# Weights of a later stage differenced during the attention, eight buffers for w3, and a reordered tail

## The chip, the core and the metric

The kernel runs on one core of a Trainium2 chip. The metric is the device time of one execution in microseconds (us). The engines named below are TensorE (PE: matmuls and transposes; its weight loads are shown as PEld), VectorE (DVE), ScalarE (ACT), GpSimd (POOL) and SyncE (SP), which issues every DMA that this text speaks of. Each engine runs its own instructions in the order in which they were laid down; between engines semaphores make an instruction wait for its operands and for buffers to come free.

## The reference

Causal attention with a bias is followed by two feed-forward blocks. Only the shape of the sums matters here:

```python
# q, k, v: 4 batches, 8 heads, 576 tokens, head_dim 64; T = 2304 tokens, DM = 512, DF = 1024
attn = softmax(where(causal, -1e9, q @ k.T / 8 + minimum(bias(s), 0)))
x = (attn @ v).reshape(2304, 512)
a, b = x @ w1, x @ w2                 # 512 x 1024 each
x2 = (a * b @ w3) @ w_out             # w3: 1024 x 1024, w_out: 1024 x 512
h = x2 @ w_in                         # second block, w_in: 512 x 1024
e = exp(h - max(h)); solu = h * e / (sum(e) + 1e-9)
ln = (solu - mean(solu)) / sqrt(var(solu) + 1e-6) * g_ln
out = ln @ w_out2                     # 1024 x 512
```

## The kernel before, in words

**Numbers.** A product in nearly full fp32 is made of three matmuls of the type fp32r: each operand is written as a high word (`hi`, an ACT copy, line 95) and a low word (`lo`, a DVE or POOL subtraction, line 100), and PE adds high·high, high·low and low·high. The weights arrive as raw 64-bit floats. One *job* is one piece of 128x512: SP loads 512 KB of raw bits into a `stage` buffer (L406), `to_f32` converts them (one ACT operation, L362, and three of DVE, L368, L369 and L373), and then the piece is either split into words (`split_w`) or, for weights that are needed late, written to scratch memory in HBM (`wf_scr`, `spill_job`). `pump(n)` emits n jobs and issues as many further loads as there are free stage buffers: 2 in the attention, 4 behind it.

**Stages.** (1) The attention goes over 32 heads in the list `steps`; PE's idle time there is filled by parts of `ab_unit`, which makes a = xw1 and b = xw2 for a batch and one slice of the columns, and `g = a*b` by DVE (L346), which is spilled to `g_scr`. The table `PUMP` says how many jobs belong to each step: first w1 and w2, then 16 spill jobs (8 of w_in, 8 of w_out2, the latter scaled by g_ln). (2) A stretch in which only the last batch's `ab_unit`s run (16 of them) and in which the 8 jobs of the first w_out and the first 6 of the 16 jobs of w3 are emitted (`AP3`). (3) **M**: since nothing stands between w3 and w_out, the product M = w3·w_out is formed once: 8 `m_unit`s of 24 matmuls each, 128x512 (L603), then split into `MH` and `ML`. A new pool of PSUM banks is opened ahead of M, so the first matmul of M waits until the last `g` has been read out of the old pool's banks. The remaining jobs of w3 are emitted between the units (`AM`); each `m_unit` needs two jobs' pieces `w3h` and `w3l`, of which five buffers each exist. (4) Chunks of 256 tokens, c = 0 to 8: x2 = g·M (L685), h from seven products by a Strassen-like scheme (L715), softmax and layer norm on ACT and DVE, transposes, and `out_unit` (24 matmuls of L809 each, 128x512).

**The operands of h.** The seven products take seven 128x512 operands of each half of w_in: the pieces B11, B21 and B22 themselves, and T1 = B12 - B11, T2 = B22 - T1, T3 = B22 - B12 and T4 = B21 - T2. Before the change these are made *during M*: `i_step` is called after each `m_unit`; the spilled pieces of w_in are loaded back (`wf`, 3 buffers), POOL does the subtractions (`wsub`, L868) into `s_m` and `a_m`, ACT makes the high words and DVE or POOL the low ones. With two halves that is 14 high words, 10 low words on DVE, 4 low words on POOL and 8 subtractions on POOL.

**The tail.** In most chunks the layer norm's result is transposed by DMA (`turn`, `join`). In the last one (tiles 16 and 17) PE does it: `tr2` is two groups of four transposes (L799), each followed by a high and a low word. `out_unit` of tiles 14 to 17 stands around them.

**What sets the order.** The program is written in one order, and a scheduler that simulates a timeline lays each engine's instructions down from it, so that what is written behind M can come out among M's instructions. SP's queue too is in one fixed order: a load that waits for its buffer holds what stands behind it.

Of the kernel before, what the change touches and what calls it, by code (L numbers as in the profile page):

```python
# [20 lines left out]
CW = 512  # L21
# [5 lines left out]
def tile_attention_moe(  # L27
# [44 lines left out]

    wf_scr = [dram.tile([128, CW], F32, name=f"wf_scr{i}") for i in range(16)]
    g_scr = [dram.tile([KF, 128, S], F32, name=f"g_scr{n}") for n in range(B)]
# [361 lines left out]

    def spill_job(i):
        src = w_in[i // 2 * 128:i // 2 * 128 + 128, i % 2 * 1024:i % 2 * 1024 + 1024] if i < 8 else wo2[(i - 8) * 128:(i - 7) * 128]

        def conv(raw):  # L440
            t = at.tile([128, CW], F32, tag="cst", bufs=2, name="cst")
            to_f32(raw, None, t)
            if i >= 8:
                nc.scalar.activation(out=t, in_=t, func=AF.Copy, scale=gln[:, i - 8:i - 7])
            nc.sync.dma_start(out=wf_scr[i], in_=t)

        jobs.append((src, conv))

    zz = r0.tile([128, HS], F32, tag="a_sb", bufs=2, name="zz")
# [53 lines left out]
    for f in range(KF):  # L505
        for w in range(2):
            wab_job(f, w)
    for i in range(16):
        spill_job(i)

# [6 lines left out]
    PD, FS = 10, 0.5  # L517
    PUMP = {3: 1, 5: 1, 6: 1, 10: 2, 11: 2, 12: 2, 13: 2, 14: 2, 15: 2, 16: 1, 18: 1, 19: 1, 20: 1, 21: 1, 22: 1, 23: 1, 24: 1, 25: 1, 26: 1, 27: 1, 28: 1, 29: 1, 30: 1, 31: 1, 32: 1, 33: 1}
    fill = []
# [71 lines left out]
    def w3_job(f, i):  # L591
        def dst():
            m_st[f, i] = [mp.tile([128, 4, 128], F32R, tag=f"w3{x}", bufs=5, name=f"w3{x}") for x in "hl"]
            return [flat(t) for t in m_st[f, i]]

        w_job(w3L[f, :, 1024 * i:1024 * i + 1024], dst)
# [105 lines left out]
    def x2_second(c):  # L702
# [5 lines left out]
        words(3, 7, s_m)  # L708

    def h_mm(ps, x, w, first):  # L710
        XH, XL = (t[:, XO[x]] for t in XW)
        WH, WL = IT[w]
        for k in range(2):
            for x_, w_ in ((XH, WH), (XH, WL), (XL, WH)):
                nc.tensor.matmul(  # L715
                    ps, x_[:, k], w_[:, k],
                    start=first and k == 0 and x_ is XH and w_ is WH, stop=k == 1 and x_ is XL, skip_group_check=not first,
                )
# [131 lines left out]
    wf = {}  # L850
    WORDER = [(0, 1), (0, 0), (2, 1), (2, 0), (1, 1), (1, 0), (3, 1), (3, 0)]
    WSRC = [2 * c + h for c, h in WORDER] + list(range(8, 16))

    def wf_load(i):
        if i < 16:
            wf[i] = wpool.tile([128, CW], F32, tag="wf", bufs=3, name="wf")
            nc.sync.dma_start(out=wf[i], in_=wf_scr[WSRC[i]])

    def i_words(n, j, src, eng):
        h_, l_ = (t[:, j] for t in IT[n])  # L860
        hi(h_, src)
        lo(l_, src, h_, eng)

    s_f = s_m.rearrange("p a b c -> p (a b c)")
    t1_, t2_, t3_ = s_f[:, 0:HD], s_f[:, HD:2 * HD], a_m.rearrange("p a t -> p (a t)")

    def wsub(dst, a, b):
        nc.gpsimd.tensor_tensor(out=dst, in0=a, in1=b, op=ALU.subtract)  # L868

    def i_step(f):  # L870
        j, s_ = divmod(f, 4)
        b = 4 * j
        if s_ == 0:
            wsub(t1_, wf[b], wf[b + 1])
            i_words("B11", j, wf[b + 1], V)
            wf_load(b + 3)
        elif s_ == 1:
            wsub(t2_, wf[b + 2], t1_)
            wsub(t3_, wf[b + 2], wf[b])
            i_words("T1", j, t1_, V)  # L880
            wf_load(b + 4)
        elif s_ == 2:
            i_words("B22", j, wf[b + 2], V)
            wsub(t1_, wf[b + 3], t2_)
            i_words("T3", j, t3_, G)
            wf_load(b + 5)
        else:
            i_words("B21", j, wf[b + 3], V)
            i_words("T2", j, t2_, G)
            i_words("T4", j, t1_, V)  # L890
            wf_load(b + 6)

    load_g(0)
    for i in range(3):
        wf_load(i)
    load_g(1)
    for f in range(nm[0], KF):
        m_unit(f)
        pump(AM[f])
        i_step(f)  # L900
        if f == 5:
            split_g(0)
# [7 lines left out]
    x2_second(0)  # L910
    split_g(1)
    load_g(2)
    x2_half(1, 0)
    p3 = None
    for c in range(NCH):
# [3 lines left out]
        if c == 0:  # L919
            for k in range(8):  # L920
                hi(OH[:, k], wf[8 + k])
                lo(OL[:, k], wf[8 + k], OH[:, k])
                wf_load(11 + k)
            wp.close()
            p3 = ctx.enter_context(tc.tile_pool(name="p3", bufs=1, side="right"))
# [76 lines left out]
```

## Time and profile before

| | |
|---|---|
| time, median of 3 runs | 752.63 us (750.18 to 755.14) |
| the profiled execution: its own time | 749.91 us |
| its span in the profile | 748.0 us |
| mean granted clock of PE over the span | 0.987 |
| PE busy | 719.9 us (96%) |
| DVE busy | 506.4 us (68%) |
| ACT busy | 468.4 us (63%) |
| POOL busy | 120.6 us (16%) |

The profile is one execution; its time stands 2.7 us under the median of the runs, and 1.9 us of it lie outside the span. In the span, stage (2) takes from 343 to 394.7 us, M from 394.7 to 451.0 us, the chunks the rest; the last `out_unit`s end at 744.2 us. A busy share is an average over stages with different limits.

### The profile page before, as it was taken

The page shows a single profiled execution, that of the slowest core. Times are in us where ns is not written, and L with a number is a line of the kernel's source. Part 1 is how long each engine was busy: PE and PEld are TensorE (multiplying, and loading weights), DVE is VectorE, ACT ScalarE, POOL GpSimd, SP SyncE. Part 2 cuts the span into 40 slices and gives each one's busy share as a digit, 9 for nine tenths or more (in the row PEclk, how much of TensorE's full clock was granted, in tenths as well). Part 3 has the DMA queues.
Part 4 walks back from the last instruction along what each step waited for, and adds up shares of the span by engine and source line. Part 5 has one row for each costly group of instructions (what it writes and reads, how often), then busy time and mean ns, then how long its engine had stood idle before and what let it go on. Part 6 is the DMA issues. An engine that isn't in the chain of part 4 may idle for free.

```text
span 748.0 us, 13033 instructions
## 1 busy us (share of the span) xinstructions
PE 719.9 (96%) x4682; PEld 626.5 (84%) x4682; DVE 506.4 (68%) x1255; ACT 468.4 (63%) x985; POOL 120.6 (16%) x114
## 2 busy tenths in 40 slices
PE   8889998999999999999999869999999999999997
PEld 5567978878889889989998649998888988888875
DVE  7977878998767677425985975566747366564651
ACT  4987878888876787523644535466656465564642
POOL 5032313232221231000002620000000000000000
PEclk9999999999999999999999979999999999999999
DMA  4744645567665653104757514143334152313301
GB/s 112 182 122 100 191 135 162 174 178 211 182 181 181 181 164 114 72 32 167 239 190 260 175 56 127 56 93 78 85 85 99 43 127 72 84 29 57 67 32 43
DMA packets 78100, 92.37 MB, mean 123 GB/s; under 512 B 41226, under 2 KB 52490, under 8 KB 78036
## 3 DMA queue, kind: packets, MB, share of 16 engines
q1 hardware_dynamic: 78036, 91.54, 43.2%
q8 instruction: 37, 0.61, 0.3%
q14 instruction: 27, 0.22, 0.1%
HBM read 57.47 MB, written 18.57 MB: 102 GB/s over the span
## 4 chain that ended last, share of the span: by engine, by line
PE 70%; DVE 4%; issue 2%; DMA 1%; ACT 1%; SPq 0%; POOLq 0%; DVEq 0%; ACTq 0%
PE x L685 13%; PE o L809 12%; PE b L326 11%; PE a L326 11%; PE hX L715 5%; PE av L298 3%; PE hZ L715 3%; PE tr L265 2%; PE m L603 2%; PE sc L178 2%; PE hW L715 2%; PE hY L715 2%; PE sc L179 2%; DMA stage<-in_w_dram 1%; DVE w3l L100 1%
## 5 line engine op out<-in xcount | busy, mean ns | idle before, releaser
L196 ACT ACTIVATE P<-P,STAT 128x576 f32<-128x576 f32 (+4 forms) x160 | 88.3, 554 | 34.4 <-DVE STAT L192 33.9
L100 POOL TENSOR_TENSOR QK<-qk,QK 64x1152 fp32r<-64x1152 f32 x24 | 66.5, 2774 | 169.7 <-ACT QK L95 152.5
L685 PE MATMUL x<-gl,MH 128*128 128x256 f32 x288 | 80.2, 279 | 0.0
L685 PE MATMUL x<-gh,ML 128*128 128x256 f32 x288 | 80.2, 279 | 0.0
L685 PE MATMUL x<-gh,MH 128*128 128x256 f32 x288 | 80.0, 279 | 0.0
L192 DVE CUSTOM_DVE_ANT_0 P<-sc,wmask 128x576 f32<-128x576 f32 (+4 forms) x160 | 70.7, 479 | 5.9 <-PE sc L170 3.2
L326 PE MATMUL a<-xT0h,W 128*128 128x288 f32 x256 | 59.2, 304 | 0.7 <-ACT a_sb L338 0.7
L326 PE MATMUL b<-xT0h,W 128*128 128x288 f32 x256 | 57.3, 298 | 1.5 <-DVE STAT L192 0.8
L779 DVE COPY lt<-turned 128x2048 uint16<-128x2048 uint16 x16 | 22.6, 1414 | 51.7 <-DMA turned<-half 51.7
L326 PE MATMUL a<-xT1h,W 128*128 128x288 f32 x256 | 57.2, 298 | 0.0
L809 PE MATMUL o<-OH,lh 128*128 128x512 f32 x144 | 57.1, 397 | 0.0
L809 PE MATMUL o<-OH,ll 128*128 128x512 f32 x144 | 57.0, 396 | 0.0
L809 PE MATMUL o<-OL,lh 128*128 128x512 f32 x144 | 56.9, 395 | 0.0
L326 PE MATMUL b<-xT1h,W 128*128 128x288 f32 x256 | 56.5, 294 | 0.0
L685 PEld LDWEIGHTS x<-gl,MH 128*128 128x128 f32 x288 | 54.0, 188 | 1.3
L685 PEld LDWEIGHTS x<-gh,MH 128*128 128x128 f32 x288 | 54.1, 188 | 1.1
L685 PEld LDWEIGHTS x<-gh,ML 128*128 128x128 f32 x288 | 54.0, 188 | 0.8
L298 PE MATMUL av<-PT,VT 128*64 128x64 f32 (+4 forms) x384 | 50.3, 395 | 0.0
L362 ACT ACTIVATE stage<-stage 128x512 f32<-128x512 f32 x56 | 37.6, 678 | 20.2 <-DMA stage<-in_w_dram 13.5
L346 DVE TENSOR_TENSOR g_sb<-b,a_sb 128x288 f32<-128x288 f32 x64 | 28.8, 450 | 29.3 <-PE b L326 25.7
L97 DVE COPY PT<-tr 64x128 f32<-64x128 f32 (+5 forms) x112 | 39.0, 379 | 11.7 <-PE tr L265 8.8
L298 PEld LDWEIGHTS av<-PT,VT 128*64 128x64 f32 x384 | 27.5, 137 | 22.2 <-issue 15.3
(194 smaller groups left out, 1997.9 us busy)
## 6 DMA issues: line engine op xcount, KB each, us to landing
stage<-in_w_dram SPq DMA_DIRECT2D x32, 512.0 KB
g_scr<-g_sb SPq DMA_DIRECT2D x32, 288.0 KB
stage<-in_wo_dram SPq DMA_DIRECT2D x16, 512.0 KB
qk<-in_qk_dram SPq DMA_DIRECT2D x24, 288.0 KB
QK<-QK SPq DMA_DIRECT2D x24, 288.0 KB
gl<-g_scr SPq DMA_DIRECT2D x24, 256.0 KB
out_dram<-o SPq DMA_DIRECT2D x18, 256.0 KB
VT<-in_vm_dram SPq DMA_DIRECT2D x16, 256.0 KB
```

The source lines that it names most:

```text
L97: eng.tensor_copy(out=dst, in_=src)
L100: eng.tensor_tensor(out=dst, in0=src, in1=hi_.bitcast(F32), op=ALU.subtract)
L192: mx = nc.vector.tensor_tensor_reduce(out=dst2, in0=ps_in, in1=msk, scale=-SCALE, scalar=BIG, op0=ALU.add, op1=ALU.min, accum_out=st[0:row ...
L196: ex = nc.scalar.activation(out=dst, in_=dst, func=AF.Exp, bias=st[0:rows, ti:ti + 1], scale=-1.0, accum_out=st[0:rows, 5 + ti:6 + ti],)
L298: nc.tensor.matmul(st["ps"][64 * e:64 * e + 64, 448 + c0:448 + c1], vr[:, j, e], PT[(2 * p + e) % 4][:, o + c0:o + c1], **kw,)
L326: nc.tensor.matmul(ps, w_[:, c, fs], x_[:, c, sl], start=(c == 0 and w_ is WH and x_ is XH), stop=(c == KC - 1 and w_ is WL),)
L346: nc.vector.tensor_tensor(out=g[:, sl], in0=ps, in1=st["a"], op=ALU.mult)
L362: nc.scalar.activation(out=high.bitcast(F32), in_=high.bitcast(F32), func=AF.Copy, scale=2.0 ** -112)
L685: last = nc.tensor.matmul(ps[:, a], w_[:, k, m * 128:m * 128 + 128], g_[:, k % 2], start=(k == 0 and w_ is MH and g_ is GH), stop=(k == KF ...
L715: nc.tensor.matmul(ps, x_[:, k], w_[:, k], start=first and k == 0 and x_ is XH and w_ is WH, stop=k == 1 and x_ is XL, skip_group_check=no ...
L779: nc.vector.tensor_copy(out=lt.bitcast(U16).rearrange("p (f w) -> p w f", w=2), in_=turned)
L809: nc.tensor.matmul(ps, l_[:, k], w_[:, k], start=(k == 0 and l_ is LH and w_ is OH), stop=(k == KF - 1 and l_ is LL),)
```

## The change

1. **Sums of w_in in the attention.** `spill_job` is replaced by `w_in_job` and `wo2_job`. The jobs of w_in come in the order B12, B11, B22, B21 of a half; as soon as its terms are there, each T is made by DVE (`minus`) and spilled like the plain pieces: 22 pieces of 256 KB are spilled, where there were 16 (B12 itself is spilled no more). `PUMP` has no jobs in steps 18 to 21, one in steps 22 to 29 (w_in), two in 30 to 33 (w_out2). In M the 14 operands are only loaded (`wf`, 5 buffers) and split, the low words all on DVE; 6 are written into M's loop and 8 behind it.
2. **Eight buffers** for `w3h` and for `w3l`, where there were five.
3. **The tail**: both `out_unit`s of tiles 14 and 15 are issued behind the last matmul of h, then `tr2(16)` and `tr2(17)`, then the last two `out_unit`s.
4. A smaller scratch area for dynamic DMAs, `dynamic_dma_scratch_size=1024`.

```diff
+    WN = [n + j for j in "01" for n in ("B11", "T1", "B21", "T2", "B22", "T4", "T3")]
+    WAT = {n: i for i, n in enumerate(WN)}
...
+    def w_in_job(n, j):
...
+        def minus(name, a, b):
+            t = at.tile([128, CW], F32, tag="tst", bufs=3, name="tst")
+            nc.vector.tensor_tensor(out=t, in0=a, in1=b, op=ALU.subtract)
+            spill(WAT[f"{name}{j}"], t)
+            return t
         def conv(raw):
-            t = at.tile([128, CW], F32, tag="cst", bufs=2, name="cst")
+            t = at.tile([128, CW], F32, tag="cst", bufs=4, name="cst")
             to_f32(raw, None, t)
...
+            if n != "B12":
+                spill(WAT[f"{n}{j}"], t)
+            if n == "B11":
+                w["T1"] = minus("T1", w["B12"], t)
+            elif n == "B22":
+                minus("T3", t, w["B12"])
+                w["T2"] = minus("T2", t, w["T1"])
+            elif n == "B21":
+                minus("T4", t, w["T2"])
...
-    PUMP = {3: 1, 5: 1, 6: 1, 10: 2, 11: 2, 12: 2, 13: 2, 14: 2, 15: 2, 16: 1, 18: 1, 19: 1, 20: 1, 21: 1, 22: 1, 23: 1, 24: 1, 25: 1, 26: 1, 27: 1, 28: 1, 29: 1, 30: 1, 31: 1, 32: 1, 33: 1}
+    PUMP = {3: 1, 5: 1, 6: 1, 10: 2, 11: 2, 12: 2, 13: 2, 14: 2, 15: 2, 16: 1}
+    PUMP.update((i, 1 if i < 30 else 2) for i in range(22, 34))
...
-            m_st[f, i] = [mp.tile([128, 4, 128], F32R, tag=f"w3{x}", bufs=5, name=f"w3{x}") for x in "hl"]
+            m_st[f, i] = [mp.tile([128, 4, 128], F32R, tag=f"w3{x}", bufs=8, name=f"w3{x}") for x in "hl"]
...
+    WL = [j * 7 + i for i in range(7) for j in range(2)] + list(range(14, 22))
     def wf_load(i):
-        if i < 16:
-            wf[i] = wpool.tile([128, CW], F32, tag="wf", bufs=3, name="wf")
+        if i < len(WL):
+            wf[i] = wpool.tile([128, CW], F32, tag="wf", bufs=5, name="wf")
...
-    def wsub(dst, a, b):
-        nc.gpsimd.tensor_tensor(out=dst, in0=a, in1=b, op=ALU.subtract)
-    def i_step(f):
-        j, s_ = divmod(f, 4)
-        b = 4 * j
-        if s_ == 0:
-            wsub(t1_, wf[b], wf[b + 1])
-            i_words("B11", j, wf[b + 1], V)
...
+    def wf_words(i):
+        t = wf.pop(i)
...
+        hi(h_, t)
+        lo(l_, t, h_, V)
+        wf_load(i + 5)
...
     for f in range(nm[0], KF):
         m_unit(f)
         pump(AM[f])
-        i_step(f)
+        if f < 6:
+            wf_words(f)
...
     split_g(1)
+    for i in range(6, 14):
+        wf_words(i)
...
-            out_unit(2 * c - 2)
-            if last:
-                tr2(2 * c)
-            out_unit(2 * c - 1)
+            with ExitStack() as order:
+                if last:
+                    order.enter_context(tc.issue_after(last_h[0].ins))
+                out_unit(2 * c - 2)
+                out_unit(2 * c - 1)
         if last:
+            tr2(2 * c)
             tr2(2 * c + 1)
...
-    nc = _bacc.Bacc("TRN2", target_bir_lowering=False, num_devices=1)
+    nc = _bacc.Bacc("TRN2", target_bir_lowering=False, num_devices=1, dynamic_dma_scratch_size=1024)
```

What this does to the order of the instructions is shown at three places. The first is DVE at the end of stage (2), around the last products `g_sb`. Before:

```order
L369 SCALAR_TENSOR_TENSOR stage_4707<-stage_4707 128x512
L346 TENSOR_TENSOR g_sb_4737<-b_4724,a_sb_4722 128x288
L368 TENSOR_SCALAR stage_4777<-stage_4777 128x512
L373 SCALAR_TENSOR_TENSOR stage_4707<-stage_4707 128x512
L369 SCALAR_TENSOR_TENSOR stage_4777<-stage_4777 128x512
L346 TENSOR_TENSOR g_sb_4737<-b_4754,a_sb_4752 128x288
L373 SCALAR_TENSOR_TENSOR stage_4777<-stage_4777 128x512
L346 TENSOR_TENSOR g_sb_4807<-b_4794,a_sb_4792 128x288
L346 TENSOR_TENSOR g_sb_4807<-b_4824,a_sb_4822 128x288
```

After, where the jobs of w3 are numbered from 0, so that stage_4805 holds job #8, stage_4875 job #9, stage_4971 job #10 and stage_4981 job #11:

```order
L346 TENSOR_TENSOR g_sb_4765<-b_4782,a_sb_4780 128x288
L368 TENSOR_SCALAR stage_4875<-stage_4875 128x512
L373 SCALAR_TENSOR_TENSOR stage_4805<-stage_4805 128x512
L100 TENSOR_TENSOR w3l_4974<-stage_4735,w3h_4973 128x512
L369 SCALAR_TENSOR_TENSOR stage_4875<-stage_4875 128x512
L368 TENSOR_SCALAR stage_4971<-stage_4971 128x512
L346 TENSOR_TENSOR g_sb_4835<-b_4822,a_sb_4820 128x288
L373 SCALAR_TENSOR_TENSOR stage_4875<-stage_4875 128x512
L369 SCALAR_TENSOR_TENSOR stage_4971<-stage_4971 128x512
L373 SCALAR_TENSOR_TENSOR stage_4971<-stage_4971 128x512
L368 TENSOR_SCALAR stage_4981<-stage_4981 128x512
L346 TENSOR_TENSOR g_sb_4835<-b_4852,a_sb_4850 128x288
```

Before, the last two products of g stand directly behind the conversion of job #8. With the change the conversions of jobs #9 and #10 and the first operation on job #11 stand ahead of the last product.

The second place is POOL in M: its row in the attention's last heads, the twelve rows of `i_step`, of which six are shown (the other six repeat them), and the first row of the chunks. Before:

```order
L100 TENSOR_TENSOR QK_673<-qk_3555,QK_673 64x2x576
...
L868 TENSOR_TENSOR s_m<-wf 128x512
L868 TENSOR_TENSOR a_m<-wf 128x512
L868 TENSOR_TENSOR s_m<-wf,s_m 128x512
L100 TENSOR_TENSOR IT3l<-a_m,IT3h 128x512
L100 TENSOR_TENSOR IT2l<-s_m,IT2h 128x512
L868 TENSOR_TENSOR s_m<-wf,s_m 128x512
L700 TENSOR_TENSOR s_m<-a_m 128x256 x2
```

After (L733 is what was L700):

```order
L100 TENSOR_TENSOR QK_679<-qk_3556,QK_679 64x2x576
L733 TENSOR_TENSOR s_m<-a_m 128x256 x2
```

All twelve are gone, and POOL has nothing to do in M. On DVE the splits that are written behind M come out among M's instructions, ahead of the last three operations on `ML`.

The third place is PE's tail, behind the last matmul of h (`lh` and `ll` are the words of the transposed tiles). Before:

```order
L715 MATMUL hX_7669<-IT3h_4871,XWl_4876 128x512
L809 MATMUL o_7743<-OH_5280,ll_7652 128x512
...
L799 MATMUL tr2_7773<-ident_88,so_7665 128x128 x4
L799 MATMUL tr2_7780<-ident_88,so_7665 128x128 x4
L809 MATMUL o_7787<-OH_5280,lh_7659 128x512
...
L809 MATMUL o_7787<-OH_5280,ll_7660 128x512
L799 MATMUL tr2_7817<-ident_88,so_7667 128x128 x4
L799 MATMUL tr2_7824<-ident_88,so_7667 128x128 x4
L809 MATMUL o_7831<-OH_5280,lh_7771 128x512
```

After:

```order
L844 MATMUL o_7803<-OH_5284,ll_7692 128x512
L834 MATMUL tr2_7833<-ident_94,so_7697 128x128 x4
L834 MATMUL tr2_7840<-ident_94,so_7697 128x128 x4
L834 MATMUL tr2_7849<-ident_94,so_7699 128x128 x4
L834 MATMUL tr2_7856<-ident_94,so_7699 128x128 x4
L844 MATMUL o_7863<-OH_5284,lh_7831 128x512
```

Both transposes now stand behind the whole of outputs 14 and 15, directly behind one another.

## Rows read from the trace of the kernel before

**Rows 1.** Waits of PE, 395 to 748 us: total, times, longest.

```profile
PE m L603 <- ACT w3h L95: 5.0, 1, 5.0
PE m L603 <- DVE w3l L100: 4.1, 2, 3.6
PE tr L799 <- DVE so L758: 2.8, 2, 1.4
PE m L603 <- DVE g_sb L346: 0.6, 1, 0.6
```

**Rows 2.** Windows: stretch, length, busy PE PEld DVE ACT POOL, clock, DMA share, GB/s.

```profile
220.00:300.00 80.00, 80.00 (x634) 72.64 (x634) 56.01 (x177) 62.69 (x159) 19.43 (x7) 1.00 0.52 155
394.70:428.40 33.70, 33.23 (x144) 26.87 (x144) 26.64 (x35) 17.77 (x31) 14.87 (x8) 1.00 0.66 220
428.40:442.60 14.20, 5.64 (x13) 3.97 (x13) 14.20 (x17) 6.99 (x12) 7.02 (x5) 0.64 0.35 109
```

**Rows 3.** Timeline of PE in M: start, duration, operation, wait before it.

```profile
394.70 0.50 PE L603 MATMUL m<-WOH,w3h 128*128 128x512 f32 x1 [0.62 <-DVE g_sb L346]
...
433.39 0.80 PE L603 MATMUL m<-WOH,w3h 128*128 128x512 f32 x1 [4.97 <-ACT w3h L95]
...
438.19 0.79 PE L603 MATMUL m<-WOH,w3l 128*128 128x512 f32 x1 [3.58 <-DVE w3l L100]
...
450.97 0.28 PE L685 MATMUL x<-gl,MH 128*128 128x256 f32 x1
```

**Rows 4.** Timeline of POOL and DVE in M: operations beside each other, one alone.

```profile
408.90 1.74 POOL L868 TENSOR_TENSOR a_m<-wf 128x512 f32<-128x512 f32 x1
...
411.11 1.77 DVE L100 TENSOR_TENSOR IB22l<-wf,IB22h 128x512 fp32r<-128x512 f32 x1
...
421.19 0.68 DVE L100 TENSOR_TENSOR IB21l<-wf,IB21h 128x512 fp32r<-128x512 f32 x1
```

**Rows 5.** Timeline of SP and DVE at the end of stage (2).

```profile
376.30 0.33 SPq L406 DMA_DIRECT2D stage<-in_w_dram  x1
...
379.78 0.43 DVE L368 TENSOR_SCALAR stage<-stage 128x512 uint32<-128x512 uint32 x1 [0.39 <-DMA stage<-in_w_dram]
...
381.80 0.33 SPq L406 DMA_DIRECT2D stage<-in_w_dram  x1
...
383.55 0.68 DVE L100 TENSOR_TENSOR w3l<-stage,w3h 128x512 fp32r<-128x512 f32 x1
384.26 0.33 SPq L406 DMA_DIRECT2D stage<-in_w_dram  x1
...
386.26 0.43 DVE L368 TENSOR_SCALAR stage<-stage 128x512 uint32<-128x512 uint32 x1 [0.46 <-DMA stage<-in_w_dram]
386.60 0.69 DVE L373 SCALAR_TENSOR_TENSOR stage<-stage 128x512 uint32<-128x512 uint32 x1
...
389.61 0.43 DVE L368 TENSOR_SCALAR stage<-stage 128x512 uint32<-128x512 uint32 x1 [1.35 <-DMA stage<-in_w_dram]
...
394.19 0.46 DVE L346 TENSOR_TENSOR g_sb<-b,a_sb 128x288 f32<-128x288 f32 x1 [1.61 <-PE b L326]
```

**Rows 6.** Timeline of PE in the attention, at 158.8 us.

```profile
158.82 0.33 PE L265 MATMUL tr<-ident,P 128*128 128x128 f32 x1 [0.57 <-DVE PT L97]
```

**Rows 7.** The costliest groups: POOL's operation of the attention.

```profile
L100 POOL TENSOR_TENSOR QK<-qk,QK 64x1152 fp32r<-64x1152 f32 x24 | 66.5, 2774 | 169.7 <-ACT QK L95 152.5
```

**Rows 8.** Timeline of PE, ACT and DVE in the tail.

```profile
707.31 0.39 PE L715 MATMUL hX<-IB11h,XWh 128*128 128x512 f32 x1
...
724.78 0.60 ACT L95 ACTIVATE lh<-tr 128x512 fp32r<-128x512 f32 x1 [1.47 <-PE tr L799]
725.41 0.69 DVE L100 TENSOR_TENSOR ll<-tr,lh 128x512 fp32r<-128x512 f32 x1 [0.78 <-ACT lh L95]
...
731.13 0.81 DVE L758 TENSOR_SCALAR so<-so,sv 128x1024 f32<-128x1024 f32 x1 [0.73 <-POOL sv L757]
...
743.96 0.40 PE L809 MATMUL o<-OH,ll 128*128 128x512 f32 x1
```

More of the change, by code (lines that the diff above doesn't have):

```diff
@@ L70, in tile_attention_moe @@
     const = ctx.enter_context(tc.tile_pool(name="const", bufs=1, side="left"))
-    wf_scr = [dram.tile([128, CW], F32, name=f"wf_scr{i}") for i in range(16)]
+    wf_scr = [dram.tile([128, CW], F32, name=f"wf_scr{i}") for i in range(22)]
     g_scr = [dram.tile([KF, 128, S], F32, name=f"g_scr{n}") for n in range(B)]
@@ L435, in wab_job, with spill, wo2_job, conv @@
         jobs.append(((w1, w2)[w][f], lambda raw: split_w(*dst(), raw, None, V)))
-    def spill_job(i):
-        src = w_in[i // 2 * 128:i // 2 * 128 + 128, i % 2 * 1024:i % 2 * 1024 + 1024] if i < 8 else wo2[(i - 8) * 128:(i - 7) * 128]
+    WN = [n + j for j in "01" for n in ("B11", "T1", "B21", "T2", "B22", "T4", "T3")]
+    WAT = {n: i for i, n in enumerate(WN)}
+    w_in_t = {}
+    def spill(i, t):
+        nc.sync.dma_start(out=wf_scr[i], in_=t)
+    def w_in_job(n, j):
+        c, half = j + 2 * (n in ("B22", "B21")), int(n in ("B12", "B22"))
+        src = w_in[c * 128:c * 128 + 128, half * 1024:half * 1024 + 1024]
+        def minus(name, a, b):
[3 more added lines that the diff above has]
+            return t
         def conv(raw):
-            t = at.tile([128, CW], F32, tag="cst", bufs=2, name="cst")
+            t = at.tile([128, CW], F32, tag="cst", bufs=4, name="cst")
             to_f32(raw, None, t)
-            if i >= 8:
-                nc.scalar.activation(out=t, in_=t, func=AF.Copy, scale=gln[:, i - 8:i - 7])
-            nc.sync.dma_start(out=wf_scr[i], in_=t)
-        jobs.append((src, conv))
+            w = w_in_t
+            w[n] = t
+            if n != "B12":
[7 more added lines that the diff above has]
+                minus("T4", t, w["T2"])
+        jobs.append((src, conv))
+    def wo2_job(k):
+        def conv(raw):
+            t = at.tile([128, CW], F32, tag="cst", bufs=4, name="cst")
+            to_f32(raw, None, t)
+            nc.scalar.activation(out=t, in_=t, func=AF.Copy, scale=gln[:, k:k + 1])
+            spill(14 + k, t)
+        jobs.append((wo2[k * 128:k * 128 + 128], conv))
     zz = r0.tile([128, HS], F32, tag="a_sb", bufs=2, name="zz")
@@ L507, in tile_attention_moe @@
             wab_job(f, w)
-    for i in range(16):
-        spill_job(i)
+    for j in range(2):
+        for n in ("B12", "B11", "B22", "B21"):
+            w_in_job(n, j)
+    for k in range(KF):
+        wo2_job(k)
     units = [(n, i, x) for n in range(B) for i in range(KF) for x in range(2)]
@@ L708, in x2_second @@
         words(3, 7, s_m)
+    last_h = [None]
     def h_mm(ps, x, w, first):
@@ L714, in h_mm @@
             for x_, w_ in ((XH, WH), (XH, WL), (XL, WH)):
-                nc.tensor.matmul(
+                last_h[0] = nc.tensor.matmul(
                     ps, x_[:, k], w_[:, k],
@@ L850, in tile_attention_moe @@
     wf = {}
-    WORDER = [(0, 1), (0, 0), (2, 1), (2, 0), (1, 1), (1, 0), (3, 1), (3, 0)]
-    WSRC = [2 * c + h for c, h in WORDER] + list(range(8, 16))
+    WL = [j * 7 + i for i in range(7) for j in range(2)] + list(range(14, 22))
     def wf_load(i):
-        if i < 16:
-            wf[i] = wpool.tile([128, CW], F32, tag="wf", bufs=3, name="wf")
[L857 to L865, printed above, removed]
-    def wsub(dst, a, b):
-        nc.gpsimd.tensor_tensor(out=dst, in0=a, in1=b, op=ALU.subtract)
-    def i_step(f):
-        j, s_ = divmod(f, 4)
-        b = 4 * j
-        if s_ == 0:
-            wsub(t1_, wf[b], wf[b + 1])
-            i_words("B11", j, wf[b + 1], V)
[L876 to L886, printed above, removed]
-        else:
[L888 to L891, printed above, removed]
+        if i < len(WL):
+            wf[i] = wpool.tile([128, CW], F32, tag="wf", bufs=5, name="wf")
+            nc.sync.dma_start(out=wf[i], in_=wf_scr[WL[i]])
+    def wf_words(i):
+        t = wf.pop(i)
+        if i < 14:
+            n, j = WN[WL[i]][:-1], int(WN[WL[i]][-1])
+            h_, l_ = (x[:, j] for x in IT[n])
+        else:
+            h_, l_ = OH[:, i - 14], OL[:, i - 14]
+        hi(h_, t)
+        lo(l_, t, h_, V)
+        wf_load(i + 5)
     load_g(0)
-    for i in range(3):
+    for i in range(5):
         wf_load(i)
@@ L919, in tile_attention_moe @@
         if c == 0:
[L920 to L923, printed above, removed]
+            for i in range(14, 22):
+                wf_words(i)
             wp.close()
```

## The prediction

> **What bounds the kernel now.** The page's shares come first: PE is busy for 96% of the span, so only stretches in which PE waits or runs slowly have anything to give. The waits of PE behind 395 us show where these are: 9.1 us in M, for the words of w3 that ACT and DVE make, and 2.8 us in the tail, for `so` [rows 1]. In the windows the attention (220 to 300 us) is PE's alone: 80.00 of 80.00 us busy, with DVE idle for 24 us of it; the first 144 matmuls of M go at 33.23/144 = 0.231 us each; then come 14.2 us in which DVE is busy all the time, 13 matmuls run, and the granted clock is 0.64 [rows 2]. Of the two levels (1.2 and 2.4 GHz) PE has the lower one for most of these 13: 5.64/13 = 0.434 us each. It fell behind the wait of 4.97 us.
>
> M's account: it takes from 394.70 to 450.97, 56.3 us [rows 3]. The 8 x 24 = 192 matmuls need 192 x 0.231 = 44.3. The other 12.0 are 9.1 of waits [rows 1], 13 x (0.434 - 0.231) = 2.6 for the low clock, and 0.3 of small things. Why is DVE late there? A subtraction that makes a low word takes 0.68 us alone, and 1.77 us when POOL's subtraction (1.74 us) runs beside it; here these two stand in turn [rows 4]. The words of w3 come behind the operands of h in DVE's queue, and in the window of 14.2 us it has no idle time left [rows 2].
>
> **POOL's work leaves M (part 1).** The twelve operations of POOL go, and DVE's operations return to 0.43 to 0.69 us. DVE takes four more low words, and the eight splits "behind M" aren't behind it in the emitted order: all 14 are among M's rows. Against that, the conversions that part 2 pulls ahead leave M. Some 45 operations at about 0.6 us are left (an estimate from the durations 0.43 to 0.69 [rows 4, 5]), 27 us, against some 38 us that PE needs up to the last unit. The cover is 11 us, and I put no wait inside M: the 12.0 us go.
>
> **Eight buffers, and a new wait ahead of M (part 2).** M's first matmul waits for the last `g` (L346): it started 0.51 us after that began [rows 3, 5]. In the new order of DVE the first operation (L368) on w3's job #11 stands ahead of this `g`, as do the conversions of #9 and #10. What did not matter before now does, when job #11 lands. A stage buffer comes free with the low word of the job four places earlier: the low word of #4 ended at 383.55 + 0.68 = 384.23, and the load of #8 was issued at 384.26 [rows 5]. From issue to L368 a load took 3.48, 4.46 and 5.35 us in the three of rows 5 (376.30 to 379.78, 381.80 to 386.26, 384.26 to 389.61). I take the middle one, since the queue stays about as full. So: L373 on #6 at 386.60, 0.69, then the low word of #5, 0.68, to 387.9, where #9's load is issued; it is there at 392.4. L368 on #9 (0.43), L373 on #8 (0.69) and the low word of #7 (0.68) follow, less their overlaps, to 394.1, where #11 is issued; it is there at 398.5. L368 and the product, 0.43 + 0.46, give 399.4 for M's first matmul, **4.7 us later** than 394.70. With loads of 3.48 us it is 2.8, with 5.35 it is 6.5. Behind DVE's wait stand the products of g and the words of w3; PE has only M to do and waits. After such a wait the clock may fall again: 0 if it doesn't, 2.6 if it falls for as long as before. I take half, 1.3, since the stall is as long as that of 4.97 us but not followed by a second one.
>
> The Trainium skill ("DMA: Bandwidth & Descriptors", "Anatomy of one DMA — SWDGE (gpsimd) path") fits a DMA's time as about 2.0 us plus its bytes over 436 GB/s, for the other path of issue; 512 KB would be an estimated 3.2 us, the handover's wait an estimated 2.2, and the sum some 2.5 us more. The rows here are longer, 3.48 to 5.35 us.
>
> So M ends 4.7 + 1.3 later than an M without waits, and the gain is 12.0 - 6.0 = **6.0 us**; bounds 12.0 - 2.8 = 9.2 and 12.0 - 6.5 - 2.6 = 2.9.
>
> **The attention (part 1 again).** It gets eight subtractions on DVE, 0.68 us each where alone [rows 4], 5.4 us; the same number of conversions, but in steps 30 to 33 two for one, 4 x (0.43 + 0.69 + 0.69) = 7.2 us more of DVE there [rows 5]; and six more spills of 256 KB in SP's queue, which hold up only what follows them until their tile is ready. All of this lies in stretches with 24 us of idle DVE in 80 [rows 2], and I cost it at nothing; if the cover fails it is rival D. Steps 18 to 21 lose their jobs; near 158 us PE waited 0.57 us for a copy that stood behind one of these operations [rows 6]. I take **0.5** for that, between 0 and 0.6.
>
> **The tail (part 3).** Before, PE waits twice for `so`, 2.8 us in all [rows 1]. With the change both transposes stand behind outputs 14 and 15. From 707.31, 42 matmuls of h and 48 of these outputs at some 0.23 us lead to about 728.1 [rows 8]. `so` of tile 16 is there long before. That of tile 17 was finished at 731.13 + 0.81 = 731.9; two high and two low words of tile 16, 2 x (0.60 + 0.69) = 2.6, which stood ahead of it on ACT and DVE, move behind it: 729.3. PE comes to it at 728.1 plus four transposes, 728.9, and waits 0.4. The first words of tile 16 (0.60 + 0.69) lie beside that. The gain is 2.8 - 0.4 = **2.4**; between 1.3 (the words of tile 16 come entirely bare ahead of output 16, and a little is lost with `so`) and 2.8. Part 4 costs nothing, since no DMA of POOL is in the trace's issues.
>
> **Sum.** 6.0 + 0.5 + 2.4 = 8.9 us. From the profiled execution's 749.91 that is 741.0, from the median of 752.63 it is 743.7. The profile lies at the fast end of the runs (750.18 to 755.14), so I take the middle, 751.3, for all cases: **742.4**, rounded to 742. With the bounds of the terms the gain is between 4.2 and 12.6, which from the two bases is 737.3 to 748.4.
>
> **Rivals.** A is the above, chance 0.57.
>
> B, no wait at the handover: loads land early enough, or what PE loses there is covered by later slack. For it: the loads of 3.48 us exist; against it: the three loads rose one after the other [rows 5]. Gain 12.0 + 0.5 + 2.4 = 14.9, 736.4. Chance 0.18.
>
> C, a wait goes on inside M: loads of w3 and reloads of operands share SP's queue, a reload that waits for its `wf` buffer holds the next load of w3, and the last units wait as before. For it: DVE starts M behind a stall, with jobs #10 and #11 to finish. Against it: 11 us of cover. One wait of the size of 4.97 or 3.58 [rows 3] stays, 4.3 us: gain 4.6, 746.7. Chance 0.17.
>
> D, slower: in the attention DVE becomes the bound. A subtraction that runs beside POOL's operation of 2774 ns [rows 7] may take as long as that, as those in M took 1.77 beside 1.74: 8 x 2.77 = 22.2, with 7.2 for the doubled jobs 29.4 us. Each operation that stands ahead of a softmax step delays PE, which has no slack there. D decides when more than the 8.9 us of gain show up on PE; with half of the 29.4, the time is 751.3 - 8.9 + 14.7 = 757.1, with all of it 771.8. Against it: 24 us idle in 80, POOL busy for only 19.43 of them, and PE's fill doesn't depend on the softmax [rows 2]. Chance 0.08.
>
> The Trainium skill ("SBUF — State Buffer", "Who interferes with whom") states that DVE's second port is GpSimd's too and that the lock is exclusive; it speaks for D and against moving two-operand work into a stretch where POOL works. The trace agrees in M: 1.77 against 0.68 us.
>
> That the change doesn't do what it says holds in part: the eight splits aren't behind M. It is in the sum, since their 8 x 0.68 = 5.4 us are among the 45 operations.
>
> **How the numbers follow.** The runs of before lie 0.7% apart, so about 1% can be told from no change: faster is below 745.1, slower above 760.2. A lies below 745.1 in nine of ten cases (0.52), B in all (0.18), C in few (0.03): 0.73 faster. Of D I put 0.05 above 760.2, the rest within. Range: B's time less a little, 735, to C's and the end of A, 748.5; left out are D and the edges, somewhat under 2 in 10.
>
> **What would show it.** In the profile of the changed kernel: M's first matmul near 399 us less what the attention gained, with a wait for `g_sb`, and ahead of it L368 on DVE waiting for a load; no row of POOL in M and low words of 0.7 us; no wait of PE between M's first matmul and x2; M from 394.7 on in about 50 us; one short wait for `so` in the tail, and the last output 2 to 3 us earlier against M's end. PE's busy share in 220 to 300 us stays at 1.00, or D is right. The forecast is wrong if waits for w3 remain, if M starts at 395, or if PE waits in the attention.

## The result, and the profile after

| | before | after |
|---|---|---|
| median of 9 runs | 750.78 us (749.29 to 755.14) | 744.91 us (741.62 to 747.2) |
| ratio after / before | | 0.9914, 95% interval 0.9887 to 0.9941 |
| the profiled execution | 749.91 us | 741.62 us |
| its span | 748.0 us | 739.8 us |

The change makes the kernel 0.9% faster, 6.5 us of 750.8 by the ratio (interval 4.4 to 8.5). Six more runs of the changed kernel gave 742.8 us and a ratio of 0.9880 (0.9855 to 0.9905). The two profiled executions lie 8.2 us apart in span, and these 8.2 can be laid out by stage, from the starts of rows in the two timelines:

| stretch | before | after | difference |
|---|---|---|---|
| start to the end of PE's last b | 394.08 | 394.44 | +0.36 |
| wait at M's first matmul | 0.62 | 4.46 | +3.84 |
| M, to the first matmul of x2 behind M's last | 56.27 | 46.47 | -9.80 |
| x2 to the last chunk's h | 256.34 | 256.43 | +0.09 |
| the tail, to the end of the last output | 36.88 | 34.16 | -2.72 |

The end of the last b is M's start less the wait before it, the end of the last output its last matmul's start plus 0.23 us. The rows of the changed kernel that bound its stretches behind M's start are these; those of before stand in [rows 3] and [rows 8]:

```profile
445.37 0.28 PE L718 MATMUL x<-gh,MH 128*128 128x256 f32 x1
...
701.80 0.39 PE L750 MATMUL hX<-IB11h,XWh 128*128 128x512 f32 x1
...
735.73 0.40 PE L844 MATMUL o<-OH,ll 128*128 128x512 f32 x1
```

The page's first line, and then PE's waits from 330 us on (total, times, longest), of the changed kernel:

```profile
PE 719.3 (97%) x4682; PEld 627.4 (85%) x4682; DVE 505.7 (68%) x1267; ACT 468.7 (63%) x985; POOL 99.3 (13%) x102
```

```profile
PE m L636 <- DVE g_sb L346: 4.5, 1, 4.5
PE o L844 <- DVE ll L100: 0.2, 1, 0.2
```

Beside [rows 1] the reader sees the whole result: both waits for `w3h` and `w3l` are gone, and both waits for `so`; one long wait, for `g_sb`, has taken their place. POOL lost 21.3 us of work; DVE's share hasn't moved.

The next rows are the handover, on SP, ACT, DVE and PE in order of time (start, duration, operation, the wait before it). The two loads in one row of SP are of jobs #9 and #10; the one at 393.22 is that of #11:

```profile
387.31 3.02 SPq L406 DMA_DIRECT2D stage<-in_w_dram  x2
...
393.22 0.33 SPq L406 DMA_DIRECT2D stage<-in_w_dram  x1
...
395.04 0.69 ACT L362 ACTIVATE stage<-stage 128x512 f32<-128x512 f32 x1 [2.43 <-DMA stage<-in_w_dram]
395.63 0.39 ACT L338 ACTIVATE a_sb<-a 128x288 f32<-128x288 f32 x1
...
398.05 0.43 DVE L368 TENSOR_SCALAR stage<-stage 128x512 uint32<-128x512 uint32 x1 [0.35 <-DMA stage<-in_w_dram]
398.39 0.45 DVE L346 TENSOR_TENSOR g_sb<-b,a_sb 128x288 f32<-128x288 f32 x1
...
398.90 0.79 PE L636 MATMUL m<-WOH,w3h 128*128 128x512 f32 x1 [4.46 <-DVE g_sb L346]
```

PE's last b ended at 394.44, and its product needs only this b and the last `a_sb`. It stands behind L368 on job #11, which waits for its load until 398.05; g follows at 398.39 and M at 398.90. The load of #11 took 4.83 us from issue to L368. What is new beside [rows 5] is ACT: its first operation on #10 stands ahead of the last `a_sb` and waited 2.43 us, so that `a_sb` too was ready only at 396.02, behind the last b.

The windows of the changed kernel (columns as in [rows 2]) show what followed on PE and what became of DVE:

```profile
220.00:300.00 80.00, 80.00 (x632) 72.32 (x632) 62.17 (x181) 60.76 (x154) 19.54 (x7) 1.00 0.62 182
...
398.90:405.00 6.10, 6.10 (x14) 4.79 (x15) 1.62 (x3) 1.00 (x2) 0.00 (x0) 0.50 0.56 179
398.90:428.40 29.50, 29.50 (x118) 24.16 (x119) 22.68 (x39) 17.98 (x33) 0.00 (x0) 0.90 0.83 286
428.40:446.00 17.60, 17.60 (x82) 14.68 (x81) 5.46 (x9) 3.49 (x7) 0.00 (x0) 1.00 0.19 61
```

The first 14 matmuls of M ran at the lower of the two clock levels (1.2 GHz, granted 0.50), 6.10/14 = 0.436 us each. After that PE is busy without a break, and DVE, which was busy for all of 14.2 us in the last units before, has 12 us of 17.6 free there.

The tail, and one of the eight subtractions in the attention:

```profile
205.38 0.67 DVE L450 TENSOR_TENSOR tst<-cst 128x512 f32<-128x512 f32 x1
...
721.80 0.81 DVE L793 TENSOR_SCALAR so<-so,sv 128x1024 f32<-128x1024 f32 x1 [0.73 <-POOL sv L792]
...
722.55 1.91 PE L834 MATMUL tr<-ident,so 128*128 128x128 f32 x16
724.66 0.50 PE L844 MATMUL o<-OH,lh 128*128 128x512 f32 x1 [0.20 <-DVE ll L100]
```

All 16 transposes run in one go; `so` of tile 17 ends at 722.6, when they start, and only 0.20 us are lost, for a low word.

### The profile page after: what moved, and what is told of

Read it like the earlier page. It is cut to its first block, busy times and chain, and to the rows that moved or that the text cites. A ratio compares the mean times of both kernels' runs of the same rounds, so it can differ in the third digit from the quotient of the medians.

```text
span 739.8 us, 13047 instructions
## 1 busy us (share of the span) xinstructions
PE 719.3 (97%) x4682; PEld 627.4 (85%) x4682; DVE 505.7 (68%) x1267; ACT 468.7 (63%) x985; POOL 99.3 (13%) x102
## 4 chain that ended last, share of the span: by engine, by line
PE 72%; DVE 11%; DMA 9%; ACT 3%; issue 2%; POOL 1%; SPq 1%; ACTq 0%; DVEq 0%; POOLq 0%
PE x L718 14%; PE o L844 13%; PE a L326 7%; PE b L326 7%; PE m L636 6%; DMA stage<-in_w_dram 6%; PE hX L750 5%; PE av L298 4%; PE hZ L750 3%; DMA stage<-in_wo_dram 3%; PE tr L265 3%; PE sc L178 2%; DVE P L192 2%; PE hW L750 2%; PE hY L750 2%
## 5 line engine op out<-in xcount | busy, mean ns | idle before, releaser
L231 ACT ACTIVATE P<-P,STAT 128x576 f32<-128x576 f32 x64 | 42.6, 714 | 10.7 <-DVE STAT L226 10.5
```

The source lines that it names most:

```text
L231: nc.scalar.activation(out=dst, in_=dst, func=AF.Copy, scale=r)
```

## The experiments

Eleven runs: ten further kernels, and the changed one again. The profiled executions differ ahead of M by up to 6.7 us (the last b ended between 394.1 and 400.8 us in the thirteen profiles), so stretches are compared from there: *L* below is the distance from the end of the last b to the end of the last output, in the profiled execution. It is 350.1 us before and 341.5 us after. Each ratio is to the runs of the kernel before that were made beside it (medians from 750.2 to 751.7 us), so it isn't always the quotient of two medians of the table. Part 4 is in every kernel with eight buffers and in all that start from the changed one; it was not tried alone.

| kernel | median us | ratio to before (95%) | wait at M's start | waits for w3 in M | L |
|---|---|---|---|---|---|
| before | 750.78 | | 0.62 | 9.1 | 350.1 |
| after | 744.91 | 0.9914 (0.9887 to 0.9941) | 4.46 | 0 | 341.5 |
| after, again | 742.80 | 0.9880 (0.9855 to 0.9905) | 6.84 | 0 | 342.9 |
| after, 5 buffers | 737.67 | 0.9809 (0.9781 to 0.9837) | 0.62 | 0.7 | 335.9 |
| after, 6 buffers | 736.72, one run | | 1.56 | 0 | 335.9 |
| after, 7 buffers | 743.72, one run | | 6.02 | 0 | 343.1 |
| after, held on DVE | 741.14 | 0.9848 (0.9819 to 0.9877) | 5.09 | 0 | 341.0 |
| after, held on DVE and ACT | 736.50 | 0.9813 (0.9781 to 0.9844) | 0.62 | 0 | 334.9 |
| after, PE filled | 742.96 | 0.9891 (0.9858 to 0.9924) | 1.61 behind the fill | 0 | 341.8 |
| after, 5 buffers, POOL busy | 743.19 | 0.9897 (0.9864 to 0.9929) | 0.62 | 3.8 | 341.4 |
| before + tail | 749.07, one run | | 1.32 | 8.8 | 347.7 |
| before + 8 buffers | 746.47 | 0.9926 (0.9899 to 0.9953) | 7.46 | 0 | 346.4 |
| before + 8 buffers, held | 742.83 | 0.9893 (0.9871 to 0.9915) | 0.87 | 1.8 | 340.8 |

### The changed kernel with five buffers

```diff
-            m_st[f, i] = [mp.tile([128, 4, 128], F32R, tag=f"w3{x}", bufs=8, name=f"w3{x}") for x in "hl"]
+            m_st[f, i] = [mp.tile([128, 4, 128], F32R, tag=f"w3{x}", bufs=5, name=f"w3{x}") for x in "hl"]
```

> The changed kernel with part 2 undone: five buffers for w3h and w3l again, so the conversions of jobs #9 to #11 can't stand ahead of the last g. Theory (the eight buffers cost the 4.46 us wait at the handover and, with it, 14 matmuls at half the clock, 14 x 0.2 = 2.8 us): M's first matmul starts at 394.5 to 395 us behind a wait of about 0.6, M shows no wait, the whole is 6 to 7 us faster than the changed kernel, ratio to the kernel before about 0.983. Rival (the eight buffers are what took the waits out of M): the handover is short, but waits of 3 to 9 us for w3 come back inside M, and the time is that of the changed kernel or above it, ratio 0.99 or more.

Measured: 737.67 us, 0.9809, and PE's waits from 330 us on are:

```profile
PE m L636 <- ACT w3h L95: 0.7, 1, 0.7
PE m L636 <- DVE g_sb L346: 0.6, 1, 0.6
PE o L844 <- DVE ll L100: 0.2, 1, 0.2
```

The theory holds but for a wait of 0.7 us inside M: without part 2 the changed kernel is faster by 0.7 to 1.05% (0.9809 against 0.9880 and 0.9914), 5 to 8 us, and M needs little more than five buffers once POOL is out of it. The rival's 3 to 9 us of waits didn't come.

### Six and seven buffers

The same edit with `bufs=6` and `bufs=7`.

> The changed kernel with six buffers for w3h and w3l: the conversion of one more job (#9) stands ahead of the last two g. Theory (the wait is the time by which the last load that stands ahead of g lands late): #9 lands at about 391.5 on the changed kernel's clock, ahead of the last b at 394.3, so the wait at M's start stays at 0.6 to 1 us. Rival (each buffer costs its share): 1.5 to 2.5 us.

> The changed kernel with seven buffers: the conversions of #9 and #10 stand ahead of the last g. Theory: #10 lands at about 395 on the changed kernel's clock, just behind the last b at 394.3, and its L368, L373, L369 and L373 follow, so the wait at M's start is 1.5 to 3.5 us, between those of six and eight buffers. Rival (no load ahead of g matters, the wait of 4.5 to 6.8 comes from something else that eight buffers bring): 0.6 us, or 4 us and more as with eight.

Measured: 1.56 and 6.02 us of wait. With six, one conversion ahead, it lies above the 0.6 to 1 us of the theory and just inside the 1.5 to 2.5 us of the rival, so this number alone doesn't decide between them; the load of #9 had landed ahead of the last b, as the theory has it, and no matmul of M ran at the lower clock. With seven I expected 1.5 to 3.5; what came is what eight bring, the number of the rival. The rows show the theory's cause all the same: the load of #10 was issued 2.8 us later than in the changed kernel (392.82 against 390.00) and landed 2.9 us behind the last b (394.95). DVE of that kernel shows

```profile
397.83 0.43 DVE L368 TENSOR_SCALAR stage<-stage 128x512 uint32<-128x512 uint32 x1 [1.83 <-DMA stage<-in_w_dram]
398.17 0.45 DVE L346 TENSOR_TENSOR g_sb<-b,a_sb 128x288 f32<-128x288 f32 x1
...
400.47 0.45 DVE L346 TENSOR_TENSOR g_sb<-b,a_sb 128x288 f32<-128x288 f32 x1
```

where the product at 398.17 is the last but one; three operations of 0.68 to 0.69 us each, which finish the conversions of #9 and #10, then stand ahead of the last. From six to seven buffers the wait grows by 4.5 us, from seven to eight (4.46 and 6.84) not clearly, so the price is no equal share per buffer: it appears when a load that lands behind the last b stands ahead of a g.

### The conversions held behind the last g, on DVE alone and on both engines

```diff
         m_unit(f)
-        pump(AM[f])
+        if f == 1:
+            pump(1)
+            behind.append(last_g[0].ins)
+            pump(1)
+        else:
+            pump(AM[f])
```

`last_g` is the last product, an operation of DVE, and this hold orders only what is on the same engine, so that in the first kernel ACT's order was free. In the second kernel the line is `behind.extend([last_g[0].ins, last_a[0].ins])`, with `last_a` the last `a_sb`, on ACT.

> The changed kernel with all its parts, eight buffers too, but the conversions of w3 from job #9 on are held behind the last product of g, so that only the order on DVE and ACT changes. Theory (it is the order on DVE that costs, not the buffers or their loads): M's first matmul at 394.5 to 395, no half clock, no wait in M, 6 to 7 us faster than the changed kernel, ratio to before about 0.983, the same as with five buffers within 1 us. Rival (the words of w3 are then late for the units 4 to 7, since three conversions come in one go behind the product): a wait of 2 to 5 us inside M, ratio 0.987 to 0.992.

> As the kernel with the hold on DVE, but ACT's part of the conversions from job #9 on is held behind the last a_sb as well (in the earlier one ACT's first operation on job #10 stood ahead of the last a_sb and waited 2.5 us for its load, so that the last g was late all the same). Eight buffers and their loads are as in the changed kernel. Theory (what costs is a conversion that waits for its load ahead of the last a_sb or g, on either engine): the wait at M's start is 0.6 to 0.7 us, M runs at full clock from its first matmul, the time is 6 to 8 us under the changed kernel's, ratio to before 0.979 to 0.985. Rival (it is the eight buffers' earlier loads that make all loads slower, and the handover waits for job #8 anyway): the wait stays at 3 us or more, ratio 0.985 to 0.992.

The first one missed: 5.09 us of wait stayed. ACT and DVE of that kernel show why:

```profile
404.40 0.65 ACT L363 ACTIVATE stage<-stage 128x512 f32<-128x512 f32 x1 [2.51 <-DMA stage<-in_w_dram]
404.96 0.39 ACT L338 ACTIVATE a_sb<-a 128x288 f32<-128x288 f32 x1
```

```profile
405.38 0.46 DVE L346 TENSOR_TENSOR g_sb<-b,a_sb 128x288 f32<-128x288 f32 x1 [3.00 <-ACT a_sb L338]
```

DVE was free, but the product needs `a_sb`, and that stood on ACT behind the first operation of a conversion whose load was still on its way. The order counts on both engines that the product needs. With both held the wait is 0.62 us, although the loads are no earlier: that of #11 is issued at 395.04, 0.65 us ahead of the end of the last b, as in the changed kernel (1.22 us ahead). So neither the buffers nor their loads make the wait, but the order; the window of M shows its floor:

```profile
396.31:402.00 5.69, 5.69 (x25) 4.69 (x26) 2.17 (x5) 1.94 (x3) 0.00 (x0) 1.00 0.44 151
396.31:440.00 43.69, 43.69 (x192) 36.18 (x193) 31.41 (x54) 22.14 (x39) 0.00 (x0) 1.00 0.68 230
```

192 matmuls in 43.69 us, 0.2276 each, at the full clock from the first one. With 736.5 us it has the lowest median, by 1.2 us against five buffers, which their intervals (0.9781 to 0.9844 and 0.9781 to 0.9837) don't tell apart.

### PE filled during the wait

```diff
+    dm = smalltile("dm")
+    with tc.issue_after(last_ab[0].ins):
+        for i in range(32):
+            nc.tensor.matmul(dm[:, 0:HS], wab[1][0][:, i % 4, 0:128], xT[1][0][:, i % 4, 0:HS], start=True, stop=True)
     right0.close()
```

> The changed kernel with 32 matmuls of 128x288 that nobody reads put on PE between the last b and M's first matmul (32 x 0.13 = 4.2 us), so that PE is busy while it waits for the last g. Theory (the half clock at M's start comes from PE's idle time of 4.46 us): M's first matmul still starts at about 398.9, but the granted clock stays at 1.00, the first 14 matmuls of M take 0.23 instead of 0.43 us each, M ends 2.5 to 3 us earlier than in the changed kernel. Rival (the clock falls at the change of stage whatever PE did before): the same 14 matmuls at 0.43, no gain.

Measured, in windows (the fill, M's start, all of M):

```profile
396.00:400.30 4.30, 4.30 (x33) 4.09 (x32) 3.31 (x7) 0.99 (x2) 0.00 (x0) 1.00 0.65 206
401.93:408.00 6.07, 6.07 (x27) 5.03 (x28) 1.66 (x3) 1.00 (x2) 0.00 (x0) 1.00 0.58 176
401.93:445.50 43.57, 43.57 (x192) 36.10 (x193) 28.18 (x47) 21.22 (x37) 0.00 (x0) 1.00 0.64 218
```

The clock stays at 1.00, and M takes 43.6 us instead of 46.5 (45.5 in the second profile of the changed kernel): the low clock costs 1.9 to 2.9 us, and it is PE's idle time ahead that brings it. The profiled execution as a whole didn't gain: M began 6.0 us behind the last b, not 4.5, since the last g came later, and from x2 on it took 1.65 us more, with 0.8 us of waits for `so` that the changed kernel doesn't have. The fill's worth is therefore read from the windows of M alone.

### The tail alone

The kernel before with the edit of part 3.

> The kernel before with part 3 alone (the order of the tail). Theory: from the first matmul of x2 behind M to the end it takes 2.4 to 2.7 us less than before's 293.2 us (450.97 to 744.19), PE waits 0.2 to 0.5 us in the tail instead of 2.8, and M is as before with waits of 8 to 10 us. Rival (part of the tail's 2.6 us in the changed kernel comes from the earlier parts, by moved work in the chunks): 1 us or less.

```profile
452.82 0.28 PE L685 MATMUL x<-gl,MH 128*128 128x256 f32 x1
...
743.09 0.40 PE L811 MATMUL o<-OH,ll 128*128 128x512 f32 x1
```

From the first matmul of x2 behind M to the end of the last output it is 290.5 us instead of 293.2, 2.7 us less (the changed kernel has 290.6), with 0.2 us of wait in the tail; M has its waits of 4.9 and 3.9 us as before. The tail's gain is its own. (L is only 2.4 us less, since M began behind 1.3 us of wait here, and not 0.6.)

### POOL busy in M again

The kernel with five buffers, and in M, for the first six units:

```diff
+            for x in range(2):
+                nc.gpsimd.tensor_tensor(
+                    out=s_m.rearrange("p a b c -> p (a b c)")[:, x * HD:x * HD + HD],
+                    in0=MH[:, f].bitcast(F32), in1=MH[:, f].bitcast(F32), op=ALU.subtract,
+                )
```

> The changed kernel with five buffers, and with twelve subtractions of 128x512 by POOL in M that nobody reads (two behind each of the first six units, of that unit's MH from itself), as many as the kernel before has there; DVE's and ACT's own work is unchanged. Theory (before, M waited because DVE's operations on two operands lasted 1.8 instead of 0.7 us beside POOL): DVE's low words beside a POOL row take 1.6 to 1.8 us, DVE loses about 12 us in M, and 3 to 9 us of waits for w3 come back, with the half clock behind them; 737.7 becomes 743 to 750. Rival (the waits came from DVE standing behind POOL's results and from the loads through three wf buffers, not from the longer operations): the rows are longer but PE waits for less than 2 us in M, and the time is that of five buffers within 2 us.

Measured: 743.19 us against 737.67, 5.5 more. DVE's rows beside a row of POOL, and the window in which POOL works:

```profile
422.94 2.79 POOL L914 TENSOR_TENSOR s_m<-MH 128x512 f32<-128x512 f32 x2 [3.45 <-ACT MH L95]
423.31 1.53 DVE L373 SCALAR_TENSOR_TENSOR stage<-stage 128x512 uint32<-128x512 uint32 x1
424.75 1.52 DVE L100 TENSOR_TENSOR IB22l<-wf,IB22h 128x512 fp32r<-128x512 f32 x1
```

```profile
410.00:440.00 30.00, 26.19 (x109) 20.70 (x108) 29.90 (x43) 15.79 (x28) 13.79 (x10) 0.94 0.74 243
```

DVE's own operations are the same as with five buffers, but 1.5 us long beside POOL instead of 0.7, and DVE is full: 29.90 of 30.00 us, where it was busy for 26.07 us of the same window without POOL. There are 3.8 us of waits for w3; 0.7 of them the kernel with five buffers has too, so 3.1 came back, and behind the longest, 2.54 us, seven matmuls ran at the lower clock. That is the theory's lower end: POOL's presence alone makes 3.1 us of waits, where the kernel before has 9.1. What makes the rest (DVE's splits there stand behind POOL's results, and the reloads go through three buffers) wasn't taken apart. The Trainium skill ("SBUF — State Buffer", "Who interferes with whom") says that DVE's second port and GpSimd's are one pair under an exclusive lock; 1.53 against 0.68 us agrees with it.

### Eight buffers alone, and with the hold

The kernel before with part 2, and with the hold on both engines as above.

> The kernel before with part 2 alone (eight buffers for w3h and w3l), and part 4, without which they don't fit. Theory (the buffers bring the handover's wait wherever they are; against M's waits they do little as long as POOL works there): M's first matmul waits 3.5 to 6 us for g_sb and 10 to 15 matmuls run at half clock, which costs 6 to 8 us; of M's waits of 8.5 us a part goes, since three more jobs are converted ahead; the time is that of before to 5 us more. Rival (the buffers are what takes the waits out of M): M without waits, 3 us or more faster than before.

> The kernel before with part 2 (and 4) and the conversions held behind the last g and a_sb on both engines; POOL's twelve operations in M are there. With part 2 alone M had no wait, but it began 7 us late, which gave DVE a lead. Theory (POOL's operations and that lead decide; without the lead the words of w3 are late again): M starts behind 0.6 us, and 3 to 9 us of waits for w3 come back in its last units, the time is 746 to 752. Rival (eight buffers alone take M's waits away, and part 1 wasn't needed for them): no wait above 1 us in M, about 12 us less than the kernel before, 739 to 741, and against the changed kernel with both holds (736.5) only the tail's 2.5 us are missing.

With eight buffers alone PE's waits from 330 us on are these:

```profile
PE m L603 <- DVE g_sb L346: 7.5, 1, 7.5
PE tr L799 <- DVE so L758: 2.8, 2, 1.4
```

The wait at M's start came and is longer than expected, 7.46 us; the rest of the theory fell and the rival came as written: M has no wait left although POOL works in it, and the kernel is 0.74% faster, not slower (interval 0.5 to 1.0%), 5.6 us. With the hold, DVE's lead at M's start is gone and still only 1.8 us of waits come back:

```profile
PE tr L801 <- DVE so L760: 2.8, 2, 1.4
PE m L605 <- ACT w3h L95: 1.5, 1, 1.5
PE m L605 <- DVE g_sb L346: 0.9, 1, 0.9
PE m L605 <- DVE w3l L100: 0.3, 1, 0.3
```

So here neither theory nor rival came as written: with nothing late at the handover, eight buffers without part 1 take away 7.3 of the 9.1 us. Parts 1 and 2 are two cures for the same wait. Part 1 is worth what is left: L is 340.8 here and 334.9 with part 1 and the tail; of these 5.9 us the tail is 2.7, M itself 46.65 - 43.69 = 3.0, and the wait at M's start 0.2.

### The changed kernel again

> The changed kernel unchanged, for a second profile of it and more times, since its runs spread from 741.6 to 747.2. Theory: the handover's wait differs from one execution to the next with the time that the loads of jobs #9 and #11 take (in the three profiles with eight buffers so far PE stood for 4.5 to 6 us behind the last b), so here it is 4 to 7 us, the first 10 to 16 matmuls of M run at half clock, and the distance from the last b to the end is 340 to 344 us. Rival: the spread comes from the stretch ahead of 130 us alone, and the wait is 4.5 us again.

Measured: 742.80 us, a wait of 6.84 us, L 342.9, and nine matmuls at the lower clock, one fewer than the least expected. As in the first profile, one load stands ahead of each of the last two products on DVE; both were later here:

```profile
397.03 0.43 DVE L368 TENSOR_SCALAR stage<-stage 128x512 uint32<-128x512 uint32 x1 [1.20 <-DMA stage<-in_w_dram]
397.38 0.45 DVE L346 TENSOR_TENSOR g_sb<-b,a_sb 128x288 f32<-128x288 f32 x1
...
400.24 0.43 DVE L368 TENSOR_SCALAR stage<-stage 128x512 uint32<-128x512 uint32 x1 [0.48 <-DMA stage<-in_w_dram]
400.58 0.45 DVE L346 TENSOR_TENSOR g_sb<-b,a_sb 128x288 f32<-128x288 f32 x1
```

The last b ended at 394.24, so #10 is there 2.8 us behind it and #11 6.0; in the first profile, with the last b at 394.44, it was 0.5 us (394.98) and 3.6. The handover's wait does differ between executions. The stretch ahead of M may be a second source of the runs' spread. The last b ended between 394.1 and 400.8 us in the thirteen profiles, with no order among the kernels, but these are mostly one profile for each kernel, and the two of the changed kernel lie only 0.2 us apart there. How far one kernel varies ahead of M is not shown.

## Why the prediction was right, and where it was off

The forecast was 742 us, a gain of 8.9 us, in a range of 735 to 748.5; the measured median is 744.91 and the interval of the gain 4.4 to 8.5 us. Case A came: M loses its waits, and a smaller one appears ahead of it. That the sum came so near (8.2 us between the two profiles) is in part luck: the handover cost 0.9 us less than forecast and M gave back 0.6 more (56.3 against a floor of 43.7), while the low clock cost 1.5 us more and the attention gave 0.9 less. The forecast put 0.73 on faster by over 1%; the first measurement, 0.86%, falls just within 1%, the second, 1.20%, beyond it. Term by term:

- **M's waits go.** Forecast: all 12.0 us, by the end of POOL's work. The mechanism is shown by the busy POOL: DVE's operations are 0.7 us without it and 1.5 beside it, and 3.1 us of waits return. It was only a part of the reason. In the account of part 2 the eight buffers had a price and no merit; the kernel with them and the hold, but without part 1, shows that they take 7.3 of the 9.1 us away. The sum wasn't touched by that, since the waits could go only once. M's floor is 43.7 us, not 44.3: 0.2276 us a matmul, where the first 144 of before, with M's slower start in them, had given 0.231.
- **The handover.** Forecast: #9 issued at 387.9, #11 at 394.1, M at 399.4, 4.7 us later than before. In the profile: 387.31, 393.22 and 398.90, 3.84 us more of wait. In the second profile it is 6.22 more, inside the bounds of 2.8 to 6.5. The place, the chain and the size are right; five buffers or the hold on both engines take the wait away, which shows the cause. I had seen only DVE in it; ACT's order is a second way to the same wait, as the hold on DVE alone showed. The remark against rival B that the loads rose one after the other doesn't hold: between those of [rows 5] lies that of job #6, issued at 378.21 and used at 383.20, 4.99 us.
- **The low clock behind it.** Forecast: 1.3, half of the 2.6 seen before. Measured: M took 46.47 and 45.47 us in the two profiles against the floor of 43.7, so 2.8 and 1.8. The first is a little above the upper bound of 2.6, which I should have taken as nearest, since the idle time there was about that of [rows 3].
- **The attention.** Forecast: a gain of 0.5 and no cost. The wait of 0.57 us [rows 6] is gone from the profile, but other small ones came, and the stretch to the last b was 0.36 us longer. That is within what the profiles differ there, so no gain is shown, and the term should have been zero. The subtractions cost nothing: all eight took 0.67 to 0.69 us, none beside a POOL row, and PE stayed busy for 80.00 of 80.00 us. Rival D didn't come, because DVE's place for them was free of POOL; what they would cost beside POOL's long operation there was not tried.
- **The tail.** Forecast 2.4, measured 2.72 in the profile and 2.7 for the tail alone. `so` of tile 17 was ready at 722.6, ahead of its transposes, instead of late by 0.4; what remains is 0.2 for a low word.

Rivals B and C: B's figure of 736.4 is near what five buffers gave, 737.67. C's wait inside M didn't appear in the changed kernel. The forecast's 742.4 against the median 744.91 leaves 2.5 us: of these the profiled executions explain 0.7 (8.2 instead of 8.9). The profiled run was the fastest of its nine, and the second profile, with a wait of 6.84, has an L that is 1.4 us longer, so the first may flatter the change. The rest isn't settled, as runs of one kernel spread by 5 us.

## What to carry to other kernels

More buffers are not free even where memory is: they let a scheduler put work that waits for a load ahead of an operation that the next stage waits for, and an engine in order then turns a late load into a stall of PE. Count, at each handover between stages, what stands ahead of the operation that releases the buffers, on every engine in its chain, and hold what isn't needed yet behind it. When two parts of a change cure the same wait, leaving one out may give the better kernel: here the changed kernel gained 6.5 and 9.0 us in its two measurements, and with part 2 undone 14. With both parts and the hold on both engines it gained 14 as well.

## What was new about the hardware

The idle time ahead sets whether PE starts M at the lower clock level, but in these profiles a longer one didn't bring more matmuls at it: behind 4.46 and 6.02 us all of the first 14 had it (granted 0.50 over the first 6 us), behind 5.09, 6.84 and 7.46 us the grant over M's first 6 us was 0.72, 0.67 and 0.64, and behind 0.62 and 1.56 us it was 1.00. What sets how many matmuls have the lower level was not taken apart. And the profiled executions of these kernels reach the end of the last b anywhere from 394.1 to 400.8 us; with such a spread ahead of a change, a stretch's own length in the profile says more about it than one run's time.
